# Pooled attention into a SoLU layer on one core: AV in 16 products instead of 24, and the upper halves of w_out on ScalarE

## The chip, the core and the metric

The kernel runs on one core of one Trainium2 chip. The time is the device time of one execution, in microseconds (us). The engines are PE (TensorE, with its weight loads as PEld), DVE (VectorE), ACT (ScalarE), POOL (GpSimd) and SP (SyncE), each with its own queue of instructions that it works through in order. SP issues most DMAs; ACT issues those of the start.

## The reference

```python
def attn(q, k, v):                      # [8, 8, 576, 64], float32
    k_p = k.reshape(B, H, 72, 8, D).mean(axis=3)
    v_p = v.reshape(B, H, 72, 8, D).mean(axis=3)
    scores = 1/sqrt(D) * q @ k_p.T      # 576 x 72 of each head
    a = exp(scores - max); a = a / (sum(a) + 1e-9)
    return a @ v_p
def moe(x, w_in, w_out, g_ln):          # x: [4608, 512] of all heads side by side
    h = x @ w_in                        # [4608, 1024]
    solu = h * softmax(h)
    ln = (solu - mean) / sqrt(var + 1e-6) * g_ln
    return ln @ w_out                   # [4608, 512]
```

The arithmetic is carried in pairs of float16 numbers: each float32 operand is split into an upper half (`hi`, the rounded value) and a rest (`lo`), and a product is the sum of hi·hi, hi·lo and lo·hi.

## The kernel before

There are 36 tiles of 128 rows. Each of the 8 batches has 512 query rows in four tiles of its own; its last 64 rows go with those of its neighbour into a mixed tile, so that four of the 36 tiles work on two batches in halves of 64 rows. Two batches take nine tiles.

For each batch K and V are loaded as eight rows of 64 beside each other (`load_kv`, L205, three DMAs: two of 512 KB, one of 128 KB) and added up by POOL in three steps (`pool_kv`, L237). The pooled V has 8 heads x 72 = 576 rows, which stand in five columns of blocks of 128. `v_hi` (L340, ACT) and `v_lo` (DVE) split it, and `v_put` (L353, POOL, four instructions of 128x512) lays it into the block matrices `vb`, in which zeros (the mask `own`) keep two neighbouring heads apart.

For each tile: `q_hi`, `q_lo`, a DMA transpose `q_T`; `scores` on PE; softmax on DVE and ACT (`s_max` to `e_mul`); `e_hi` (L661, ACT) and `e_lo` (L664, POOL); a DMA transpose `e_T` (L670); `av` (L676, PE); `x_hi`, `x_lo`; `mm1` (L704, 24 products of 512 columns in three parts); the SoLU and its norm (`h_max`, `h_exp`, `z_mul`, `z_cen`, `z_hi`, `z_lo`); two DMA transposes `z_T`; `mm2` (L817, 24 products of 512 columns); `o_evac` and `o_store`. A pair of heads has 144 rows of V, more than the 128 of a block, and lies across two blocks. So `av` takes, for each of the four pairs, two blocks times the three half products: 24 products of 128 columns, 48 of 64 columns in a mixed tile.

At the start the weights w_in and w_out are loaded in four pieces each and bounded, scaled and split: `w_exp`, `w_shift`, `w_bnd`, `w_tail`, `w_sgn`, `w_mul`, then `w_dg` (L533) and `w_hi` (L522) and on PE `w_res` (L543, two buffers `ps_h` shared with `mm1`), then `w_lo`. For w_in `w_hi` is on ACT; for w_out `w_hi` and `w_dg` are on DVE, beside POOL's work. `k_dup` (L302) is ACT's first computation.

The order is planned when the kernel is built: `op(...)` gives every step its engine, a cost in us, a due time (moved by the table `SHIFT`) and what it depends on; `plan` (L886) lays the steps out engine by engine, twelve rounds, and the best plan is issued in its order. A DMA's completion is counted on one of eight counters, taken in turn by every DMA of SP and ACT (`DMAHW0` to `DMAHW7` in the listings below). A DMA that takes a counter whose earlier user hasn't landed waits for it in its queue, and what stands behind it in that queue waits too.

```python
                todo = [(e, et, vt) for e in range(2) for et, vt in PASSES]
                for j, (e, et, vt) in enumerate(todo):
                    nc.tensor.matmul(
                        xp[:, c, lo:hi],
                        lhsT=vb[b % 2][:, vt, c, e].rearrange("p j d -> p (j d)"),
```

## Time and profile before

| what | us |
|---|---|
| median of 3 runs (lowest to highest) | 546.53 (545.97 to 548.0) |
| the profiled execution | 546.37 |
| its span, first to last instruction | 544.6 |
| around the span | 1.77 |
| PE busy | 494.2 (91%) |
| DVE busy | 420.4 (77%) |
| POOL busy | 322.3 (59%) |
| ACT busy | 316.8 (58%) |

The profile is of one execution. An engine's busy time is how long it had an instruction at work; the chain that ended last is followed back from the last instruction, at each step to what released it. The granted clock of TensorE is given as a share of 2.4 GHz. A wait is put down to what came last.

### The profile page before, as it was taken

What the parts mean: (1) busy time and instruction counts of PE and PEld (TensorE: products, weight loads), DVE (VectorE), ACT (ScalarE), POOL (GpSimd) and SP (SyncE); (2) the same over time, 40 slices, a digit from 0 to 9 for tenths busy, and PEclk for the clock granted to TensorE, in tenths of its full rate; (3) what the DMA queues carried; (4) which work ended last, traced back from release to release, by engine and by line L of the source; (5) the groups of instructions that cost most, each with busy time, mean ns of one, the idle gap of its engine ahead of it and who ended that gap; (6) DMA issues with size and microseconds to landing.
All of it is one profiled execution on the core that took longest, in us unless ns stands there. A gap on an engine that the chain in (4) does not pass through costs nothing.

```text
span 544.6 us, 9825 instructions
## 1 busy us (share of the span) xinstructions
PE 494.2 (91%) x3558; PEld 268.2 (49%) x3558; DVE 420.4 (77%) x901; ACT 316.8 (58%) x449; POOL 322.3 (59%) x417
## 2 busy tenths in 40 slices
...
GB/s 329 341 144 181 272 39 65 168 228 166 82 261 177 178 102 159 151 251 117 159 240 163 137 134 158 193 194 89 222 207 176 132 86 124 144 95 82 84 77 78
DMA packets 191936, 86.90 MB, mean 160 GB/s; under 512 B 168336, under 2 KB 176528, under 8 KB 191376
## 3 DMA queue, kind: packets, MB, share of 16 engines
...
q8 instruction: 28, 0.46, 0.4%
q14 instruction: 20, 0.16, 0.1%
...
## 4 chain that ended last, share of the span: by engine, by line
PE 67%; DVE 11%; DMA 10%; issue 4%; ACT 3%; SPq 2%; POOL 2%; ACTq 0%; POOLq 0%; DVEq 0%
PE hp L714 26%; PE op L826 25%; PE xp L684 7%; PE sc L616 3%; DMA vr<-in_v_dram 2%; DMA qr<-in_q_dram 2%; DMA eT<-e 2%; DMA qm<-in_q_dram 2%; DMA qT<-q 2%; PE res_wo L547 1%; PE res_wi L547 1%; DVE z L759 1%; DVE wo L527 1%; DVE m L724 1%; PE kTp L310 1%
## 5 line engine op out<-in xcount | busy, mean ns | idle before, releaser
L714 PE MATMUL hp<-wi,xT 128*128 128x512 f16 x864 | 200.0, 379 | 2.4 <-ACT xT L693 2.4
L826 PE MATMUL op<-wo,zT 128*128 128x512 f16 x864 | 198.7, 379 | 1.7 <-ACT osb L834 1.7
L779 POOL TENSOR_TENSOR z<-z,z 128x512 f16<-128x512 f32 x71 | 82.8, 1180 | 112.6 <-ACT z L773 99.8
L826 PEld LDWEIGHTS <-zT 128*128 128x128 f16 x864 | 83.0, 98 | 96.3 <-issue 2.5
L714 PEld LDWEIGHTS <-xT 128*128 128x128 f16 x864 | 82.7, 98 | 95.5 <-ACT xT L693 3.2
L666 POOL TENSOR_TENSOR e<-e,e 128x576 f16<-128x576 f32 x36 | 48.7, 1353 | 51.3 <-ACT e L662 51.3
L724 DVE TENSOR_REDUCE m<-hp 128x1 f32<-128x1024 f32 x36 | 43.9, 1220 | 24.1 <-PE hp L714 24.0
L735 ACT ACTIVATE z<-hp,nb,Hb 128x1024 f32<-128x1024 f32 x32 | 38.4, 1201 | 39.3 <-DVE nb L727 37.0
L684 PEld LDWEIGHTS <-vb 128*128 128x128 f16 x960 | 51.2, 98 | 10.1 <-DMA eT<-e 3.0
L684 PE MATMUL xp<-eT,vb 128*128 128x128 f16 (+1 forms) x960 | 54.4, 214 | 1.9 <-DMA eT<-e 1.7
L768 ACT ACTIVATE z<-z,sz 128x1024 f32<-128x1024 f32 x36 | 41.2, 1145 | 21.8 <-DVE z L759 21.6
L759 DVE SCALAR_TENSOR_TENSOR z<-hp,rs,z 128x1024 f32<-128x1024 f32 x36 | 46.0, 1279 | 4.0 <-ACT z L735 2.9
L246 POOL TENSOR_TENSOR kr<-kr 128x512 f32<-128x512 f32 (+3 forms) x48 | 42.4, 901 | 8.7 <-DMA kr<-in_k_dram 7.3
L246 POOL TENSOR_TENSOR vr<-vr 128x512 f32<-128x512 f32 (+3 forms) x48 | 42.6, 908 | 6.8 <-DMA vr<-in_v_dram 6.5
L693 ACT ACTIVATE xT<-xp 128x512 f16<-128x512 f32 x36 | 21.4, 594 | 41.7 <-PE xp L684 41.7
L662 ACT ACTIVATE e<-e 128x576 f16<-128x576 f32 x36 | 24.5, 680 | 30.0 <-DVE e L656 29.0
L626 DVE TENSOR_REDUCE mx<-sc 128x8 f32<-128x576 f32 x36 | 27.1, 753 | 18.8 <-PE sc L616 18.2
L773 ACT ACTIVATE z<-z 128x1024 f16<-128x1024 f32 x36 | 37.9, 1054 | 0.9
L792 ACT ACTIVATE junk<-z 128x1024 f16<-128x1024 f32 x36 | 37.5, 1043 | 0.7 <-POOL wor L422 0.7
L355 POOL TENSOR_TENSOR vb<-v,own 128x512 f16<-128x512 f16 x32 | 35.8, 1142 | 1.5 <-ACT v L343 1.5
L834 ACT ACTIVATE osb<-op,f 128x512 f32<-128x512 f32 x36 | 24.5, 681 | 19.4 <-PE op L826 9.2
L616 PE MATMUL sc<-kT,qT 128*128 128x72 f16 (+1 forms) x640 | 27.4, 201 | 5.1 <-DMA qT<-q 4.8
(240 smaller groups left out, 641.6 us busy)
## 6 DMA issues: line engine op xcount, KB each, us to landing
...
kr<-in_k_dram SPq DMA_DIRECT2D x14, 512.0 KB, 4.6
qr<-in_q_dram SPq DMA_DIRECT2D x14, 512.0 KB, 4.2
vr<-in_v_dram SPq DMA_DIRECT2D x14, 512.0 KB, 5.3
wir<-in_moe_w_in_dram ACTq DMA_DIRECT2D x4, 1024.0 KB, 12.0
...
zT<-z SPq DMA_TRANSPOSE x72, 2.8
kr<-in_k_dram ACTq DMA_DIRECT2D x2, 512.0 KB, 3.8
```

What stands on the lines that cost most here:

```text
L246: nc.gpsimd.tensor_tensor(out=dst, in0=src[:, :, :n], in1=src[:, :, n : 2 * n], op=ALU.add)
L616: nc.tensor.matmul(o, lhsT=t["qT"][:, h, lo:hi], rhs=kT[:, x, h * SP : (h + 1) * SP], start=(x == 0), stop=(x == 1),)
L666: nc.gpsimd.tensor_tensor(out=eh[:, 1, :NR], in0=tl[i]["e"], in1=eh[:, 0, :NR], op=ALU.subtract)
L684: nc.tensor.matmul(xp[:, c, lo:hi], lhsT=vb[b % 2][:, vt, c, e].rearrange("p j d -> p (j d)"), rhs=eT[:, et * NC + c + e, lo:hi], start=(j ...
L714: nc.tensor.matmul(hp[:, f], lhsT=xT[:, xt, c], rhs=wi[:, wt, c, f * 512 : (f + 1) * 512], start=(c == 0 and xt == 0 and wt == 0), stop=(c ...
L724: nc.vector.tensor_reduce(out=small(i, "m"), in_=tl[i]["hp"], axis=AX.XY, op=ALU.max)
L735: nc.scalar.activation(z, t["hp"], AF.Exp, bias=t["nb"], scale=hsc(i, 0), accum_out=small(i, "se"))
L759: nc.vector.scalar_tensor_tensor(out=t["z"], in0=t["hp"], scalar=t["rs"], in1=t["z"], op0=ALU.mult, op1=ALU.mult, accum_out=small(i, "sz"),)
L768: nc.scalar.activation(t["zf"], t["zf"], AF.Identity, bias=t["sz"], scale=-float(DFF))
L773: nc.scalar.activation(t["z16"][:, 0], t["zf"], AF.Copy)
L779: eng.tensor_tensor(out=t["z16"][:, 1, fs], in0=t["zf"][:, fs], in1=t["z16"][:, 0, fs], op=ALU.subtract)
L826: nc.tensor.matmul(op_, lhsT=zT[:, zt, c], rhs=wo[:, wt, c], start=(c == 0 and zt == 0 and wt == 0), stop=(c == CO - 1 and zt == 1),)
```

## The change

AV is laid out anew. V is loaded by pairs of heads: of the 144 rows of a pair the first 128 make a block of their own (four blocks, columns 0 to 3 of `vp`), and the last 16 of all four pairs share two more blocks (columns 4 and 5), in which each set of 16 rows stands four times. Their split is laid out so that one product takes hi·hi, hi·lo and lo·hi of the rest at once: the copies of V hold hi or lo (`v_sel` makes the per-partition scale, `v_hi` is now two instructions), those of e hold hi, hi, lo, zero (`e_hi` and `e_lo` are now two instructions each). So a pair takes three products for its block and one for the rest: 16 in all, 32 of 64 columns in a mixed tile. The third piece of V's load becomes eight DMAs of 16 partitions and 64 KB each, `pool_kv` of that piece works on 128 partitions and two columns instead of 64 and one, and `v_put` is three instructions.

`w_hi` and `w_dg` of w_out (and `w_dg` of w_in) move from DVE to ACT. The first two pieces of w_in are loaded into the room of `wo`, and the pool `raw` has 6 buffers instead of 7. The planner gets the new costs, and a surcharge for four kinds of DVE step when POOL is at work (`LOCK`), and the table `SHIFT` is new.

```diff
 SHIFT = {
-    "a_all.k": -7.29,
+    "a_all.k": -21.62,
...
-    raw = ctx.enter_context(tc.tile_pool(name="raw", bufs=7))
+    raw = ctx.enter_context(tc.tile_pool(name="raw", bufs=6))
...
+    PIECES = {"kr": ((0, 2), (2, 4), (4, 5)), "vr": ((0, 2), (2, 4), (4, 6))}
...
+        if which == "vr":
+            pairs = rows.rearrange("(t r) x -> r t x", r=PR)
+            if part < 2:
+                eng.dma_start(t[:, c0:c1], pairs[:P, c0:c1])
+            else:
+                for n in range(8):
+                    eng.dma_start(t[16 * n : 16 * n + 16, c0:c1], pairs[P:, n // 4 :: 2])
...
+    def v_sel(b):
+        st = bat[b]
+        st["ss"] = sm.tile([P, 1], F32, tag="ss", name=f"ss{b}")
+        nc.vector.tensor_scalar(
+            out=st["ss"], in0=sel, scalar1=grp["v", b]["s"], scalar2=None, op0=ALU.mult
+        )
...
+        cs = slice(0, CI) if n == 0 else slice(CI, NV)
+        nc.scalar.activation(
+            st["v2"][:, 0, cs], vp[b % 2][:, cs], AF.Copy,
+            scale=grp["v", b]["s"] if n == 0 else st["ss"],
+        )
...
+    HOME = (("wi", 0), ("wi", 1))
...
-                nc.vector.tensor_scalar(
-                    out=w_dst(nm, c, 0)[:, d], in0=w_f32(nm, c)[:, d],
-                    scalar1=w_scl(nm, 2 * c + d), scalar2=None, op0=ALU.mult,
+                nc.scalar.activation(
+                    w_dst(nm, c, 0)[:, d], w_f32(nm, c)[:, d], AF.Copy,
+                    scale=w_scl(nm, 2 * c + d),
                 )
...
-            nc.vector.tensor_scalar(
-                out=t[:, d], in0=ident, scalar1=w_scl(nm, 2 * c + d), scalar2=None, op0=ALU.mult
-            )
+            nc.scalar.activation(t[:, d], ident, AF.Copy, scale=w_scl(nm, 2 * c + d))
...
+    def e_hi(i, n):
+        m, r_ = e_dst(i)
+        if n == 0:
+            nc.scalar.activation(m[:, 0], e_pair(i)[:, :, :P], AF.Copy)
+        else:
+            nc.scalar.activation(
+                r_[:, :, 0:2], e_pair(i)[:, :, P:].unsqueeze(2).to_broadcast([P, CI, 2, 16]), AF.Copy
+            )
...
-                todo = [(e, et, vt) for e in range(2) for et, vt in PASSES]
-                for j, (e, et, vt) in enumerate(todo):
+                for n, (x, e) in enumerate(((0, c), (1, c), (0, CI + c), (2, 2 * CI + c // 2))):
                     nc.tensor.matmul(
...
+    LOCK = ("w_shift", "w_dg", "h_bat", "h_mix")
```

In the listings that follow a row is a line number, an instruction, and out<-in by the program's names; what it waits for stands in brackets. The first place is ACT's queue at the start of the program, up to its first computation (`vr0` is batch 0's V, `wir` w_in, `kp` the pooled K). Before:

```order
L370 DMA wir1_136<-in_moe_w_in_dram 128x2048
L212 DMA vr0_138<-in_v_dram 128x2x512
L212 DMA vr0_138<-in_v_dram 128x2x512 [waits DMAHW0_49]
L216 DMA vr0_138<-in_v_dram 64x512 [waits DMAHW1_49]
L370 DMA wir2_143<-in_moe_w_in_dram 128x2048 [waits DMAHW2_49]
L370 DMA wir3_145<-in_moe_w_in_dram 128x2048 [waits DMAHW3_49]
L477 DMA g_sb_103<-in_moe_g_ln_dram 128x8x1 [waits DMAHW4_49]
L303 ACT_TABLE_LOAD
L303 ACTIVATE kp_0_87<-kp_0_87 128x5x64 [waits Pool_49]
```

After, from the fourth of V's eight small pieces on:

```order
L240 DMA vr0_140<-in_v_dram 16x2x512 [waits DMAHW4_49]
L240 DMA vr0_140<-in_v_dram 16x2x512 [waits DMAHW5_49]
L240 DMA vr0_140<-in_v_dram 16x2x512 [waits DMAHW6_49]
L240 DMA vr0_140<-in_v_dram 16x2x512 [waits DMAHW7_49]
L240 DMA vr0_140<-in_v_dram 16x2x512 [waits DMAHW0_49]
L424 DMA wir2_152<-in_moe_w_in_dram 128x2048 [waits DMAHW1_49]
L424 DMA wir3_154<-in_moe_w_in_dram 128x2048 [waits DMAHW2_49]
L531 DMA g_sb_104<-in_moe_g_ln_dram 128x8x1 [waits DMAHW3_49]
L333 ACT_TABLE_LOAD
L333 ACTIVATE kp_0_87<-kp_0_87 128x5x64 [waits Pool_49]
```

Twenty DMAs instead of thirteen stand ahead of ACT's first computation, and twelve of them instead of five wait on a counter. The last four small pieces wait for the first two pieces of w_in and the two large pieces of V, which stand eight places earlier; the last two pieces of w_in and `g_sb` wait for small pieces.

The second place is SP's queue around the loads of batch 5 (`vr5` is its V, `qm2` the mixed rows of q, `zT`, `qT`, `eT` the transposes with their tile's number). Before:

```order
L212 DMA vr5_3332<-in_v_dram 128x2x512 [waits DMAHW1_49]
L212 DMA vr5_3332<-in_v_dram 128x2x512 [waits DMAHW2_49]
L216 DMA vr5_3332<-in_v_dram 64x512 [waits DMAHW3_49]
L230 DMA qm2_3339<-in_q_dram 64x8x64 [waits DMAHW4_49]
L230 DMA qm2_3339<-in_q_dram 64x8x64 [waits DMAHW5_49]
L787 DMA_TRANSPOSE zT15_3359<-z16_15_3342 128x8x128 [waits DMAHW6_49,Activation_49]
L842 DMA out_0_dram<-osb13_3354 64x512 [waits DMAHW7_49,Activation_49]
L842 DMA out_0_dram<-osb13_3354 64x512 [waits DMAHW0_49]
L603 DMA_TRANSPOSE qT20_3401<-q16_20_3208 128x8x128 [waits DMAHW1_49,DVE_49,PE_49]
L673 DMA_TRANSPOSE eT17_3407<-e16_1_95 128x10x128 [waits DMAHW2_49,Pool_49]
```

After, where the two large pieces of V and four small ones stand just ahead:

```order
L240 DMA vr5_3319<-in_v_dram 16x2x512 [waits DMAHW7_49]
L240 DMA vr5_3319<-in_v_dram 16x2x512 [waits DMAHW0_49]
L240 DMA vr5_3319<-in_v_dram 16x2x512 [waits DMAHW1_49]
L240 DMA vr5_3319<-in_v_dram 16x2x512 [waits DMAHW2_49]
L857 DMA_TRANSPOSE zT15_3352<-z16_15_3342 128x8x128 [waits DMAHW3_49,Activation_49]
L857 DMA_TRANSPOSE zT15_3352<-z16_15_3342 128x8x128 [waits DMAHW4_49,Pool_49]
L655 DMA_TRANSPOSE qT20_3407<-q16_20_3141 128x8x128 [waits DMAHW5_49,DVE_49,PE_49]
L745 DMA_TRANSPOSE eT18_3433<-e16_0_95 128x10x128 [waits DMAHW6_49,Pool_49]
```

Ten DMAs of V instead of three stand ahead of the transposes, and the last small pieces wait on the counters of the large ones.

The third place is where w_out's scale `sg_wo` has been found. Before, on DVE (`nb` and `pz` belong to tile 1's SoLU):

```order
L507 TENSOR_SCALAR sg_wo<-g_sb,sw_wo 128x8
L538 TENSOR_SCALAR dg_wo_682<-ident,sg_wo 128x128 x2
L527 TENSOR_SCALAR wo<-wor_255,sg_wo 128x512 x2
L727 TENSOR_SCALAR nb_689<-m_649,Hb_390 128x1
L742 TENSOR_SCALAR pz_699<-nb_689 128x1
```

After, on ACT (`z_622` is tile 0's SoLU, `q_4` a split of q, `sg_wo_645` signs of w_out, `xT` AV's result):

```order
L805 ACTIVATE z_622,se_623<-hp_540,nb_618,Hb_420 128x1024
L473 ACTIVATE sg_wo_645<-wor_298 128x1024
L592 ACTIVATE dg_wo_650<-ident,sg_wo 128x128 x2
L581 ACTIVATE wo<-wor_268,sg_wo 128x512 x2
L643 ACTIVATE q_4_679<-qm_391,sq('m', 0)_487 128x8x64
L473 ACTIVATE sg_wo_691<-wor_296 128x1024
L763 ACTIVATE xT_696<-xp_655 128x512
L581 ACTIVATE wo<-wor_271,sg_wo 128x512 x2
```

The scale's first users leave DVE's queue and stand in ACT's, between tile 0's exponential and the work of the next tiles.

## Rows read from the trace of the kernel before

**Rows 1.** The page's first part: busy time, share of the span, instructions.

```profile
PE 494.2 (91%) x3558; PEld 268.2 (49%) x3558; DVE 420.4 (77%) x901; ACT 316.8 (58%) x449; POOL 322.3 (59%) x417
```

**Rows 2.** Stretches: length, busy us of PE, PEld, DVE, ACT, POOL; clock, DMA, GB/s.

```profile
60.00:80.00 20.00, 10.10 (x34) 4.88 (x33) 16.65 (x31) 7.21 (x9) 17.63 (x21) 0.72 0.44 128
80.00:100.00 20.00, 17.83 (x88) 8.92 (x87) 18.22 (x48) 12.30 (x18) 5.15 (x4) 0.77 0.28 59
...
220.00:240.00 20.00, 20.00 (x166) 10.84 (x165) 18.63 (x40) 13.49 (x20) 17.78 (x24) 1.00 0.82 192
...
100.00:520.00 420.00, 417.02 (x3128) 228.25 (x3126) 333.21 (x742) 256.44 (x377) 252.92 (x338) 1.00 0.71 157
```

**Rows 3.** The chain that ended last: start us, us, what.

```profile
154.59 1.34 PE xp L684 x24
...
466.44 1.40 PE xp L684 x48
```

**Rows 4.** In order of time: start, us, engine, line, tiles [idle <-releaser].

```profile
9.24 0.39 ACTq L477 DMA_DIRECT2D g_sb<-in_moe_g_ln_dram  x1
...
9.66 1.28 ACT L303 ACT_TABLE_LOAD   x1 [9.66 <-DMA qr<-in_q_dram]
...
11.65 1.14 ACT L381 ACTIVATE u_wi<-wir 128x1024 f32<-128x1024 f32 x1 [0.23 <-DMA wir<-in_moe_w_in_dram]
...
15.48 2.94 POOL L246 TENSOR_TENSOR vr<-vr 128x512 f32<-128x512 f32 x2 [5.17 <-DMA vr<-in_v_dram]
```

**Rows 5.** The chain that ended last, 15 to 79 us.

```profile
15.31 8.82 DMA qT<-q
...
57.64 8.83 DMA qm<-in_q_dram
...
70.99 2.13 DVE dg_wo L538 x2
73.12 5.58 DVE wo L527 x2
```

**Rows 6.** In order of time: first mm1, exponential of tile 1, upper halves.

```profile
51.72 5.35 PE L714 MATMUL hp<-wi,xT 128*128 128x512 f16 x24 [0.78 <-ACT xT L693]
...
78.92 1.20 ACT L735 ACTIVATE z<-hp,nb,Hb 128x1024 f32<-128x1024 f32 x1 [7.65 <-DVE nb L727]
...
83.15 0.88 DVE L527 TENSOR_SCALAR wo<-wor,sg_wo 128x512 f16<-128x512 f32 x2
```

**Rows 7.** Groups by line: shapes xcount | busy us, mean ns | idle before.

```profile
L693 ACT ACTIVATE xT<-xp 128x512 f16<-128x512 f32 x36 | 21.4, 594 | 41.7 <-PE xp L684 41.7
...
L662 ACT ACTIVATE e<-e 128x576 f16<-128x576 f32 x36 | 24.5, 680 | 30.0 <-DVE e L656 29.0 <-DMA qT<-q 1.0
...
L303 ACT ACTIVATE kp<-kp 128x320 f32<-128x320 f32 x8 | 3.7, 464 | 6.1 <-POOL kp L246 6.0
```

**Rows 8.** SP's queue in order of time, around the loads of batch 5.

```profile
274.86 1.08 SPq L212 DMA_DIRECT2D vr<-in_v_dram  x2
275.99 0.50 SPq L216 DMA_DIRECT2D vr<-in_v_dram  x1
...
280.19 1.26 SPq L787 DMA_TRANSPOSE zT<-z  x1
```

**Rows 9.** DMA issues: queue, count, KB of each, median us to landing.

```profile
kr<-in_k_dram SPq DMA_DIRECT2D x14, 512.0 KB, 4.6
...
vr<-in_v_dram SPq DMA_DIRECT2D x14, 512.0 KB, 5.3
...
kr<-in_k_dram SPq DMA_DIRECT2D x7, 128.0 KB, 5.4
...
eT<-e SPq DMA_TRANSPOSE x36, 3.5
```

**Rows 10.** A transpose of e on SP's queue, and the AV that waits for it.

```profile
284.23 1.37 SPq L673 DMA_TRANSPOSE eT<-e  x1
...
289.18 1.51 PE L684 MATMUL xp<-eT,vb 128*128 128x128 f16 x24 [1.49 <-DMA eT<-e]
```

More of the change, by code (lines that the diff above doesn't have):

```diff
@@ L39 @@
+    "a_scale.v": 9.35,
+    "av": 0.2,
+    "e_T": -35.76,
+    "e_hi": 0.79,
+    "e_lo": 5.3,
     "e_mul": 8.03,
-    "e_rec": -0.94,
+    "e_rec": -1.23,
     "e_sum": -0.71,
-    "g_all": 3.07,
-    "g_max": -7.17,
-    "g_par": -0.13,
-    "h_bat": -7.02,
-    "h_exp": 10.98,
-    "h_max": -0.22,
-    "h_mix": 5.51,
-    "k_T": 6.76,
-    "k_dup": -0.29,
-    "k_hi": -10.23,
-    "k_lo": 0.24,
-    "load_kv": -3.11,
-    "load_q": -2.51,
-    "mm1": 1.89,
-    "mm2": 17.69,
-    "n_f": -6.27,
@@ L58 @@
-    "n_u": 0.28,
-    "o_evac": 1.32,
-    "o_store": 19.63,
-    "pool_kv": 2.95,
-    "q_T": 0.49,
-    "q_hi": 1.92,
-    "q_lo": -0.97,
-    "s_exp": -0.25,
-    "s_max": -1.15,
-    "s_scale": -18.57,
-    "s_sub": -15.94,
-    "v_hi": -8.55,
-    "v_put": -9.46,
-    "w_all.wi": 4.98,
-    "w_all.wo": 0.91,
-    "w_bnd.wi": 21.74,
-    "w_bnd.wo": 11.25,
-    "w_dg.wi": -1.48,
-    "w_dg.wo": -9.92,
-    "w_exp.wi": 3.61,
-    "w_exp.wo": -0.14,
-    "w_hi.wi": 1.44,
-    "w_hi.wo": 0.16,
@@ L103 @@
-    "z_cen": -3.7,
-    "z_hi": 2.72,
-    "z_lo": -0.21,
-    "z_mul": -2.61,
-    "z_var": -13.56,
+    "g_all": -0.73,
+    "g_max": -5.26,
+    "g_par": -5.5,
+    "h_bat": -1.1,
+    "h_exp": 16.71,
+    "h_max": -0.53,
+    "h_mix": 5.41,
+    "h_nb": 12.08,
+    "k_T": 7.39,
+    "k_dup": -5.05,
+    "k_hi": -18.66,
+    "k_lo": -0.62,
+    "load_g": 2.84,
+    "load_kv": 13.41,
+    "load_q": -1.14,
+    "load_qm": 5.52,
+    "mm1": 6.24,
+    "mm2": 17.69,
+    "n_f": -7.69,
+    "n_u": 12.93,
@@ new lines @@
+    "o_evac": 2.32,
+    "o_store": 18.59,
+    "pool_kv": 3.34,
+    "q_T": 8.03,
+    "q_hi": 1.3,
+    "q_lo": -1.2,
+    "s_exp": 17.42,
+    "s_max": -1.08,
+    "s_scale": -27.59,
+    "s_sub": -21.86,
+    "scores": -1.24,
+    "v_hi": -10.93,
+    "v_put": -10.2,
+    "v_sel": 0.46,
+    "w_all.wi": -1.93,
+    "w_all.wo": -2.71,
+    "w_bnd.wi": 7.93,
+    "w_bnd.wo": 11.25,
+    "w_dg.wi": -3.34,
+    "w_dg.wo": -11.46,
+    "w_exp.wi": -0.35,
+    "w_exp.wo": 1.16,
+    "w_hi.wi": 2.97,
@@ new lines @@
+    "w_hi.wo": -0.18,
+    "w_lo.wi": -8.77,
+    "w_lo.wo": -3.33,
+    "w_load": 2.82,
+    "w_mul.wi": -23.05,
+    "w_mul.wo": 8.49,
+    "w_par.wi": 15.48,
+    "w_par.wo": -0.82,
+    "w_res.wi": -11.03,
+    "w_res.wo": 1.46,
+    "w_rmax.wi": -9.29,
+    "w_rmax.wo": -8.02,
+    "w_sgn.wi": -4.96,
+    "w_sgn.wo": 9.07,
+    "w_shift.wi": -1.82,
+    "w_shift.wo": 1.26,
+    "w_tail.wi": 0.65,
+    "w_tail.wo": -13.63,
+    "wi_scale": 3.13,
+    "wo_scale": -7.86,
+    "x_hi": -0.18,
+    "x_lo": -12.0,
```

200 lines of the change are left out of this document (109 added, 91 removed).

## The prediction

> **What bounds the kernel now.** I read the page's busy times first, then the busy times by stretch, then the chain that ended last, and then, where PE stands idle, the engines in order of time. By the page PE is busy 494.2 of 544.6 us, DVE 420.4 [rows 1]. By stretch this falls into two programs. From 100 to 520 us PE is busy 417.0 of 420 us [rows 2]; nothing else is as full, and the chain there is a row of products. What leaves PE in that stretch leaves the time, until another engine is full. The nearest is DVE with 333.2 of 420, and 18.63 of 20 in its fullest stretch [rows 2]. Before 100 us PE is not the bound: 10.10 of 20 us from 60 to 80, at a mean granted clock of 0.72 (a mixture of the two levels 2.4 and 1.2 GHz), while DVE has 16.65 and then 18.22 [rows 2]. There DVE, its waits and POOL beside it set the pace.
>
> **AV.** A tile's 24 products take 1.34 us in the chain, a mixed tile's 48 take 1.40 [rows 3]: 55.8 and 29.2 ns each. Eight fewer in 32 tiles are 32 x 8 x 0.0558 = 14.3 us, sixteen fewer in four mixed tiles 4 x 16 x 0.0292 = 1.9: 16.2 in all. Two of the tiles (2 x 0.45) come before PE is full, which leaves 15.3 us on the path. The trace shows no product over a block of rests, but its shapes are those of the others, so the price holds.
>
> The Trainium skill, TensorE: Matmul & The Clock Gate, section Back-to-back issue gap, has about 81 ns for such a product of 128 columns in a stream of weight loads and products; the row has 55.8, and the measurement decides. By the page's figure an estimate of the saving would be 32 x 8 x 0.081 + 4 x 16 x 0.081 = 25.9 us.
>
> **What the rests add to the other engines.** e_hi was one instruction of 0.680 us; now one of 512 columns, nearest 0.594, and one of 128, at most the 0.464 of 320 columns [rows 7]: up to 0.38 us more of ACT for each tile, 13.6 in all, on an engine that is busy 256.4 of 420 us from 100 to 520 [rows 2]. On POOL (252.9 of 420) e_lo grows by an instruction, v_put shrinks from four to three and the sums of V's last piece double; all of this is under a us for each tile, and PE's work on other tiles hides it. If that cover were gone, e's transposition, and so AV, would come about 0.5 us later. I take 0.
>
> **V's loads and SP's queue.** Three DMAs of V become ten. In the trace two took SP 1.08 us, the third 0.50 [rows 8], and the next transposition stood behind 1.6 us of V. A large piece of V lands 5.3 us after its issue [rows 9]. The last two small pieces wait on the counters of the two large ones, so the queue is free again no earlier than about 5.3 + 2 x 0.50 = 6.3 us: 4.7 more, in six batches that are loaded while PE is full. Behind it stand z, q and e transposes, and PE for them. The trace has one place where e is late: its transpose was issued at 284.23, right behind such loads, and AV began at 289.18 after PE had waited 1.49 us [rows 10]; had it landed in the median 3.5 us [rows 9], PE would not have waited. PE lost almost nothing elsewhere (3.0 of 420 us, rows 2), so mostly there is room. Bounds: 0, and 6 x 1.6 = 10 if a third of each delay is seen. I take +3, nearer the first, since the plan puts z's transposes, not e's, behind most of these loads.
>
> In the trace a piece of 128 KB lands after 5.4 us, one of 512 KB after 4.6 [rows 9]. The Trainium skill, DMA: Bandwidth & Descriptors, section Rules for kernel authors, speaks against such a split: join small transfers, under 64 KB is mostly overhead. Rows and rule agree that a small piece saves no time in landing; by the rule alone the term would be the upper bound, 10, and the sum 7 us worse.
>
> **DVE when PE is faster.** 420 us become about 405 for the same 333 us of DVE, so its fullest stretch of 18.63 in 20 [rows 2] becomes 19.3. Some steps will come late: bounds 0 and 5, I take +2.
>
> **The start, first half: a loss.** ACT's first computation was at 9.66, when the DMA of g_sb, waiting for q's second half, had been issued at 9.24 [rows 4]. Now small pieces wait in ACT's queue for w_in's pieces and V's. V's first large piece landed about 15.5, when POOL began on it, and the second by about 16.9, in the middle of POOL's two steps of 2.94 [rows 4]. Behind that stand four issues (the last small piece, two of w_in, g_sb) of some 0.4 us [rows 4]: ACT begins at about 18.5, 8.9 us later. Not all of it is lost, because q's first transposition took 8.82 us from 15.31 on [rows 5], behind w_in's pieces; now it is issued at about 24.3 (18.5 + 1.28 for the table + 0.46 for k_dup + 1.14 for an exponent step + 0.7 for q_hi [rows 4, 7] + 2.2 on DVE), those pieces have landed, and at the 3.5 of e's transpose [rows 9] it is there at about 27.8 instead of 24.1: +3.7. The new order gives ACT about 3.3 us more between w_in's scale and the first mm1 (two exponent steps of w_out, second halves of e_hi and v_hi, w_dg), so the first mm1 starts some 7 us after its 51.72 [rows 6].
>
> **The start, second half: a gain.** DVE stood waiting for qm's DMA, 8.83 us from 57.64 to 66.47 [rows 5], since its issue was behind K's and V's loads. Now qm is issued ahead of them. Then DVE spent 2.13 + 5.58 = 7.7 us on one pair of w_dg and two halves of w_hi [rows 5], beside a busy POOL; two such halves took 0.88 once POOL was idle [rows 6]. Tile 1's exponential waited 7.65 us for what stood behind them on DVE [rows 6]. On ACT the same four steps cost 2 x 0.46 + 2 x 0.594 = 2.1 [rows 7], 5.6 less. Adding up DVE's steps in the new order I get w_out's scale at about 68.4 instead of 71.0, so w_hi is through at 70.5 instead of 78.7: 8.2 earlier. Part is given back: ACT, at 7.21 and 12.30 of 20 us [rows 2], takes 4 x 2.1 = 8.4 us there, and two buffers serve w_res and mm1 in turn. Half of 8.2 is 4; less 1, because the first half's delay may not be hidden to the end, I take -3 for the whole start. Bounds: -10 (8.2 and the 2.6 of the scale, nothing given back) and +8 (the first half's 7 and an us of lower clock).
>
> **The sum.** -15.3 + 3 + 2 - 3 = -13.3 from the profiled execution's 546.37 is 533.1; its time stands 0.16 under the median of 546.53, so I say 533.
>
> **The rivals.**
> - *The whole gain of the start.* DVE's waits beside POOL vanish and ACT hides its loads: -16.2 - 10 + 2 = about 522. For it: the 7.7 us of rows 5. Against: ACT's 8.9 us.
> - *The start loses.* The delay of 7 reaches the second half and PE falls to 1.2 GHz again after idling, as it did from 60 to 80: -15.3 + 3 + 2 + 8 = -2.3, 544. For it: ACT's queue. Against: PE was half idle there before, too, so a late mm1 costs little of itself.
> - *Slower: SP's queue becomes the bound.* Every delay of 4.7 us by V's ten DMAs is seen by PE at six batches, 28 us: -15.3 - 3 + 28 = +10, about 556. It is a loss from (15.3 + 3) / 6 = 3.1 us a batch on. For it: the place of rows 10. Against: PE's 417 of 420.
> - *DVE becomes the bound,* and half of AV's gain stays: -7.7 - 3 + 5 = -5.7, 541.
> - *A product costs more than the chain shows,* by the figure cited above: 25.9 instead of 15.3 in the sum, -23.9, 522. No row of the trace bears it out.
>
> **How the numbers follow.** Forecast 0.60; the start's whole gain 0.14; the start loses 0.12; SP 0.06; DVE 0.06; the product's price 0.02. A measurement of this kernel tells about 0.5% from no change, here 543.8 to 549.3. The forecast, the two cases at 522, DVE's and a third of the start's loss lie below: 0.60 + 0.14 + 0.02 + 0.06 + 0.04 = 0.86. Two thirds of the start's loss are no change, 0.08; SP is slower, 0.06. The range leaves out SP, part of the start's loss and the best of its gain: 521 to 544.
>
> **What would show it.** Right: AV's row at 16 products in about 0.9 us, 32 in 0.93; PE still busy 99% from about 100 us on, that stretch shorter by 10 to 15 us; ACT's table load near 18.5; the first mm1 near 58, w_out's first w_hi near 70. Wrong: PE waits on eT, zT or qT summing to over 10 us, each with V's small pieces before it on SP (the slower rival); DVE at 19 of 20 for long with PE waiting for it; or a first mm1 after 62, with PE's clock at 0.5 once mm2 has begun.

## The result and the profile after

The changed kernel takes 539.19 us (median of 4 runs, 537.49 to 540.55) beside 546.51 of the kernel before: a ratio of 0.986, 95% interval 0.9825 to 0.9895. That is 7.3 us less, where 13.5 were forecast (533 in a range of 521 to 544). The profiled execution took 538.74 us, its span is 537.0. Medians are of all runs of a kernel, ratios of its fast runs alone; only the last experiment (best) has a slow run, of 535.66 us, and the median of its other five is 530.51.

The page of the kernel after, busy time of each engine; the answer to [rows 1]:

```profile
PE 475.5 (89%) x3238; PEld 251.6 (47%) x3238; DVE 417.0 (78%) x895; ACT 330.3 (62%) x510; POOL 323.5 (60%) x445
```

PE has 18.7 us less to do, but the span is only 7.6 us shorter: PE stands idle for 61.5 instead of 50.4 us. Where, the stretches tell (columns as in [rows 2]). First the start of the kernel before, which was not shown:

```profile
0.00:100.00 100.00, 58.23 (x347) 31.71 (x348) 82.71 (x149) 53.80 (x64) 64.62 (x74) 0.90 0.62 189
```

Then the same and the rest, after:

```profile
0.00:100.00 100.00, 49.33 (x331) 28.79 (x332) 78.54 (x137) 55.31 (x78) 60.81 (x74) 0.93 0.65 189
...
60.00:80.00 20.00, 11.00 (x86) 6.96 (x87) 19.27 (x29) 6.71 (x11) 13.81 (x15) 0.79 0.43 108
80.00:100.00 20.00, 17.69 (x116) 9.99 (x116) 18.73 (x44) 18.49 (x32) 11.30 (x14) 0.87 0.25 46
...
100.00:520.00 420.00, 414.92 (x2860) 218.09 (x2859) 337.74 (x758) 270.28 (x427) 260.12 (x368) 1.00 0.80 166
```

Idle time of PE before 100 us: 41.8 before, 50.7 after. From 100 to 520 us: 3.0 before, 5.1 after. The start can be cut at the first mm1, as the prediction cuts it. Before:

```profile
0.00:51.72 51.72, 22.52 (x167) 13.52 (x167) 39.58 (x63) 30.66 (x34) 36.99 (x47) 1.00 0.79 255
51.72:100.00 48.28, 35.71 (x180) 18.19 (x181) 43.13 (x87) 23.14 (x30) 27.63 (x27) 0.79 0.45 118
```

After:

```profile
0.00:63.65 63.65, 23.22 (x169) 14.33 (x169) 44.19 (x70) 31.39 (x38) 39.27 (x49) 0.98 0.87 268
63.65:100.00 36.35, 26.11 (x162) 14.46 (x163) 34.35 (x68) 23.92 (x41) 21.53 (x26) 0.85 0.27 51
```

Up to the first mm1 PE is idle for 29.2 us before and 40.4 after; from there to 100 us for 12.6 and 10.2. AV's own row, in the chain that ended last (start, us, what), answers to [rows 3]:

```profile
142.93 0.89 PE xp L755 x16
...
234.12 0.93 PE xp L755 x32
```

The groups of instructions by line give AV 39.8 us of PE in all, 54.4 before. Set against the sum of the prediction, in us of the profiled span:

| part | forecast | rows of both traces |
|---|---|---|
| AV's products | -15.3 | 39.8 - 54.4 = -14.6 |
| PE's waits from 100 to 520 us (SP's queue +3, DVE +2) | +5 | 5.1 - 3.0 = +2.1 |
| start, first half: PE idle up to the first mm1 | +1 | 40.4 - 29.2 = +11.2 |
| start, second half: PE idle from there to 100 us, and PE's other work | -4 | 10.2 - 12.6 - 4.1 = -6.4 |
| end, behind 520 us | 0 | +0.2 |
| sum | -13.3 | -7.5 |

The 4.1 are what is left of PE's 18.7 beside AV: with the same instructions, work done at a higher mean clock (0.93 instead of 0.90 before 100 us), most of it `w_res` of w_out (12.6 us of PE instead of 16.2). The two lines of the start make +4.8 together, where -3 was forecast: the miss is the start, and in it the first half. Its rows, in order of time (start, us, engine, line, tiles [idle before <-releaser]); they answer to [rows 4 to 6]:

```profile
5.75 12.52 ACTq L240 DMA_DIRECT2D vr<-in_v_dram  x8
...
19.73 1.28 ACT L333 ACT_TABLE_LOAD   x1 [19.73 <-DMA vr<-in_v_dram]
...
63.65 5.80 PE L784 MATMUL hp<-wi,xT 128*128 128x512 f16 x24 [0.47 <-ACT xT L763]
...
67.48 5.72 DVE L699 TENSOR_SCALAR r<-r 128x8 f32<-128x8 f32 x1
...
79.37 2.06 DVE L561 TENSOR_SCALAR sg_wo<-g_sb,sw_wo 128x8 f32<-128x8 f32 x1
...
82.06 1.40 ACT L581 ACTIVATE wo<-wor,sg_wo 128x512 f16<-128x512 f32 x2
```

ACT's table load came at 19.73 (18.5 forecast, 9.66 before). The first mm1 came at 63.65 (some 58.7 forecast, 51.72 before). w_out's first upper half came at 82.06, where the forecast had both through by 70.5. And a step of DVE on 8 columns, e_rec, lasted 5.72 us, where its median is 0.17.

### The profile page after: what moved, and what is told of

It is laid out like the page before. It is cut to its first block, busy times and chain, and to the rows that moved or that the text cites. A ratio compares the mean times of both kernels' runs of the same rounds, so it can differ in the third digit from the quotient of the medians.

```text
span 537.0 us, 9335 instructions
## 1 busy us (share of the span) xinstructions
PE 475.5 (89%) x3238; PEld 251.6 (47%) x3238; DVE 417.0 (78%) x895; ACT 330.3 (62%) x510; POOL 323.5 (60%) x445
## 4 chain that ended last, share of the span: by engine, by line
PE 52%; DVE 13%; DMA 11%; POOL 8%; issue 4%; ACT 4%; SPq 2%; POOLq 0%; ACTq 0%; DVEq 0%
PE hp L784 20%; PE op L896 20%; DMA vr<-in_v_dram 6%; PE xp L755 4%; POOL vr L276 2%; PE sc L668 2%; DVE z L829 2%; DMA eT<-e 2%; POOL z L849 1%; DVE r L699 1%; PE res_wi L599 1%; POOL kr L276 1%; DMA kr<-in_k_dram 1%; PE res_wo L599 1%; DVE q L647 1%
## 5 line engine op out<-in xcount | busy, mean ns | idle before, releaser
L784 PE MATMUL hp<-wi,xT 128*128 128x512 f16 x864 | 196.1, 380 | 0.6 <-ACT xT L763 0.6
L896 PE MATMUL op<-wo,zT 128*128 128x512 f16 x864 | 194.2, 380 | 2.2 <-ACT osb L904 1.7
L849 POOL TENSOR_TENSOR z<-z,z 128x512 f16<-128x512 f32 x71 | 84.0, 1198 | 83.8 <-ACT z L843 71.7
L734 POOL TENSOR_TENSOR e<-e,e 128x512 f16<-128x512 f32 x36 | 43.6, 1211 | 27.6 <-ACT e L725 27.5
L276 POOL TENSOR_TENSOR vr<-vr 128x512 f32<-128x512 f32 (+1 forms) x48 | 49.8, 1052 | 12.4 <-DMA vr<-in_v_dram 10.1
L829 DVE SCALAR_TENSOR_TENSOR z<-hp,rs,z 128x1024 f32<-128x1024 f32 x36 | 46.1, 1281 | 5.3 <-ACT z L805 4.4
L755 PE MATMUL xp<-eT,vb 128*128 128x128 f16 (+1 forms) x640 | 39.8, 219 | 6.4 <-POOL vr L276 3.2
L755 PEld LDWEIGHTS <-vb 128*128 128x128 f16 x640 | 36.5, 100 | 15.4 <-issue 4.2
L725 ACT ACTIVATE e<-e 128x512 f16<-128x512 f32 x36 | 22.5, 625 | 28.5 <-DVE e L708 28.4
L767 DVE SCALAR_TENSOR_TENSOR xT<-xp,xT 128x512 f16<-128x512 f32 x36 | 24.7, 686 | 11.9 <-ACT xT L763 11.6
```

The costliest lines, as they stand in the source:

```text
L276: nc.gpsimd.tensor_tensor(out=dst, in0=src[:, :, :n], in1=src[:, :, n : 2 * n], op=ALU.add)
L734: nc.gpsimd.tensor_tensor(out=m[:, 1], in0=e_pair(i)[:, :, :P], in1=m[:, 0], op=ALU.subtract)
L755: nc.tensor.matmul(xp[:, c, lo:hi], lhsT=vb[b % 2][:, x, c].rearrange("p j d -> p (j d)"), rhs=eT[:, e, lo:hi], start=(n == 0), stop=(n == 3),
L784: nc.tensor.matmul(hp[:, f], lhsT=xT[:, xt, c], rhs=wi[:, wt, c, f * 512 : (f + 1) * 512], start=(c == 0 and xt == 0 and wt == 0), stop=(c ...
L829: nc.vector.scalar_tensor_tensor(out=t["z"], in0=t["hp"], scalar=t["rs"], in1=t["z"], op0=ALU.mult, op1=ALU.mult, accum_out=small(i, "sz"),)
L849: eng.tensor_tensor(out=t["z16"][:, 1, fs], in0=t["zf"][:, fs], in1=t["z16"][:, 0, fs], op=ALU.subtract)
```

## The experiments

Two theories on the start: A, it is lost in ACT's queue behind V's small pieces; B, it is lost on DVE, held beside POOL. Two more questions: what AV's products are worth in the end, and whether SP's queue and the new order took a part. The kernel before was run again beside the experiments, with medians of 546.46 to 546.98; single runs of a kernel lie 2 to 4 us apart, so a difference of 2 us between two medians is no more than the scatter. Wherever the listing says nothing else, the order of the operations is that of the changed kernel.

### What AV is worth: av24 and b_av16

```diff
-for n, (x, e) in enumerate(((0, c), (1, c), (0, CI + c), (2, 2 * CI + c // 2))):
+todo = ((0, c), (1, c), (0, c), (1, c), (0, CI + c), (2, 2 * CI + c // 2))
+for n, (x, e) in enumerate(todo):
...
-    rhs=eT[:, e, lo:hi], start=(n == 0), stop=(n == 3),
+    rhs=eT[:, e, lo:hi], start=(n in (0, 2)), stop=(n in (1, 5)),
```

> The changed kernel with 24 products in AV again: the first two of each block are computed twice, the second time with a fresh start of the sum, so that the output stays and the order, the loads and the other engines' work are those of 16. If PE is the bound after 100 us and a product costs what the chain shows, 32 x 8 x 0.0558 + 4 x 16 x 0.0292 = 16.2 us come back and the whole is about 554. If DVE, SP or the loads had become the bound after the change, a part of it would be hidden: under 10 us, below 549.

549.48 us, 10.3 more than the changed kernel and 2.7 more than the kernel before (ratio 1.0051, 1.0032 to 1.0071). The stretches of av24, the start and the full part:

```profile
0.00:100.00 100.00, 49.45 (x351) 29.85 (x352) 77.45 (x136) 54.45 (x77) 61.07 (x73) 0.93 0.64 189
100.00:520.00 420.00, 418.15 (x3103) 228.03 (x3102) 331.22 (x745) 266.35 (x421) 255.72 (x363) 1.00 0.79 164
```

PE is busy 490.9 us, 15.4 more: the price of a product was right. But PE now idles 1.9 us from 100 to 520 instead of 5.1, so 3.2 of the 15.4 had been given back as waits. That leaves 12 us between the two profiled executions, and 10.3 between the medians. And with 24 products the new kernel is the slower one: all that the change does beside AV costs about 2.7 us. The forecast had +2 for it, by two errors of opposite sign (below).

In the kernel before, the other way:

```diff
-todo = [(e, et, vt) for e in range(2) for et, vt in PASSES]
+todo = [(e, et, vt) for e in range(2) for et, vt in PASSES[:2]]
```

> The kernel before, with 16 of its 24 products in AV: the third pass, the lower halves of V against the upper halves of e, is left out; all else, the order and the loads too, is the kernel before. If the chain's 55.8 ns a product are what a product costs on the path, the whole falls by 15.3 to 16.2 us from 546.5 to about 531. If DVE or a transfer is next as soon as PE has less to do, a part of it is lost, and the whole falls by about 10, to 536, as the changed kernel rose by 10 with 24 products.

By `PASSES` the pass that is left out is the other one, e's lower halves against V's upper ones; the number of products is the same.

540.74 us: only 5.7 less (0.9894, 0.9867 to 0.9921), less than either case. The stretch from 100 us on, and two of PE's waits:

```profile
100.00:520.00 420.00, 410.39 (x2858) 216.71 (x2856) 337.81 (x746) 256.83 (x379) 254.98 (x340) 1.00 0.72 159
...
237.16 3.63 PE L714 MATMUL hp<-wi,xT 128*128 128x512 f16 x16 [1.11 <-ACT xT L693]
289.82 1.89 PE L684 MATMUL xp<-eT,vb 128*128 128x128 f16 x16 [2.84 <-DMA eT<-e]
```

PE idles 9.6 us there instead of 3.0, and the place of [rows 10] waits 2.84 instead of 1.49 us. In the old order, what stood just in time for a full PE is late as soon as PE has less to do. The order was not planned anew for 16 products here.

### What the new order is worth: old_table

The table `SHIFT` of the kernel before in the changed kernel.

> The changed kernel with one part undone: the table that sets the planner's order is that of the kernel before; the operations, their durations and the loads are those of the changed kernel. The kernel before with 16 products fell by 5.7 us where the changed kernel rose by 10.3 with 24. If the new table is what lets the rest of AV's saving through, the whole is 4 to 6 us longer, 542 to 545. If the new table only moves the work, and the start's loss comes from it, the whole is 2 to 5 us shorter, 534 to 537.

550.8 us, 11.6 more than the changed kernel, and slower than the kernel before (1.0072, 1.0042 to 1.0101). PE idles 12.1 us from 100 to 520 us, 7.0 more than in the changed kernel; another 1.5 us of idle time come before 100 us, and PE's work takes 3.6 us longer. The longest wait from 100 us on stands behind V's loads. SP's queue and the AV that waits:

```profile
396.87 5.53 SPq L232 DMA_DIRECT2D vr<-in_v_dram  x8
402.58 1.26 SPq L849 DMA_TRANSPOSE zT<-z  x1
403.94 1.18 SPq L904 DMA_DIRECT2D out_dram<-osb  x2
405.20 1.56 SPq L737 DMA_TRANSPOSE eT<-e  x1
...
410.41 1.05 PE L747 MATMUL xp<-eT,vb 128*128 128x128 f16 x16 [3.22 <-DMA eT<-e]
```

So the order is a part of this change: under the old table the change loses.

### What SP's hold costs: v_16

```diff
-    eng.dma_start(t[16 * n : 16 * n + 16, c0:c1], pairs[P:, n // 4 :: 2])
+    for c in range(1 if b == 0 else 2):
...
+        eng.dma_start(t[16 * n : 16 * n + 16, cs], pairs[P:, ts])
```

Here `cs` and `ts` are one chunk each from the second batch on.

> The changed kernel, but from the second batch on the small pieces of V are sixteen of 32 KB instead of eight of 64 KB, each chunk by itself; the bytes are the same. In the changed kernel eight such issues held SP 6.32 us at 59.16; sixteen wait for the landings of the eight before, and hold it some 5 to 6 us more for each of seven batches. If SP's hold is on the path as the prediction priced it (3 us for 4.7 us in each of six batches), the whole is 3 to 5 us longer, 542 to 544; by the slower rival, where every us of it is seen, over 25 us longer; if it is hidden, within 1.5 us of 538.7.

565.94 us (1.034, 1.0306 to 1.0375), 26.7 more, about what the slower rival had. One of the seven places, and PE's work behind it:

```profile
416.91 9.61 SPq L243 DMA_DIRECT2D vr<-in_v_dram  x16
426.62 1.26 SPq L860 DMA_TRANSPOSE zT<-z  x1
427.98 1.36 SPq L748 DMA_TRANSPOSE eT<-e  x1
...
431.59 1.86 PE L758 MATMUL xp<-eT,vb 128*128 128x128 f16 x16 [4.72 <-DMA eT<-e]
433.25 7.21 PE L899 MATMUL op<-wo,zT 128*128 128x512 f16 x24
```

PE's stretches there (columns as in [rows 2]):

```profile
431.00:434.00 3.00, 2.41 (x18) 1.99 (x19) 0.00 (x0) 0.51 (x2) 0.00 (x0) 0.50 0.89 231
434.00:441.00 7.00, 7.00 (x41) 3.27 (x39) 3.65 (x11) 2.55 (x6) 6.13 (x11) 0.78 1.16 197
```

In the changed kernel the small pieces hold SP for 46.2 us in seven batches (5.24 to 8.61 each), here for 72.9 (9.61 to 11.61): 26.7 more, and the whole is 26.7 longer. That the two are the same number is chance. PE's idle time from 100 to 520 us goes from 5.1 to 20.4, 15.3 us for 26.7 of hold; nearly all of the rest is PE's longer busy time, 10.8 us. Behind the wait of 4.72 us the granted clock is 0.50 (1.2 GHz) from 431 to 434 and 0.78 from 434 to 441, and mm2's 24 products took 7.21 us instead of 5.34. So the hold of 6.6 us for each batch is hidden but for a few us in all, and over half of what v_16 adds to it is seen as waits. These are two points: where between 6.6 and 10.4 us for each batch the waits begin wasn't tried. The longest wait in the changed kernel from 100 us on stands behind the pieces of V that held SP from 394.50 on:

```profile
394.50 6.66 SPq L240 DMA_DIRECT2D vr<-in_v_dram  x8
401.26 1.27 SPq L857 DMA_TRANSPOSE zT<-z  x1
402.63 1.38 SPq L745 DMA_TRANSPOSE eT<-e  x1
...
406.29 1.05 PE L755 MATMUL xp<-eT,vb 128*128 128x128 f16 x16 [2.18 <-POOL vr L276]
```

The wait is put down to a sum of V on POOL, which AV doesn't read; e's transpose, at its median of 3.5 us, landed at about 406.1, and is the likelier cause.

### ACT's queue at the start: v_sp0 and v_spq

```diff
 for n, _, _ in order:
-    ops[n][3](*ops[n][4])
+    fn, args = ops[n][3], ops[n][4]
+    if fn is load_kv and args[1:] == (0, "vr", 2):
+        continue
+    fn(*args)
+    if fn is load_g:
+        load_kv(nc.sync, 0, "vr", 2)
```

> The changed kernel, but the eight small pieces of V of the first batch are issued from SP, which stands idle at the start, instead of from ACT. Theory A (the start is lost in ACT's queue, where those eight issues took 12.52 us from 5.75 on): ACT's table load falls from 19.73 to about 10 to 12, the first mm1 from 63.65 to about 55 to 57, and the whole from 538.7 to about 533. Theory B (the start is lost on DVE beside POOL, where e_rec took 5.72 us at 67.48 and w_out's scale 2.06 at 79.37): ACT begins earlier, but the first w_hi of w_out stays near 80 and the whole within 2 us of 538.7.

538.63 us, no difference. It doesn't decide between the theories: the counters that a DMA waits for go round over SP's and ACT's DMAs together, so ACT's own loads came to wait instead, and the table load stood at 17.32, behind w_in. The first mm1 came 2.3 us earlier, at 61.32, but PE's waits from 100 to 520 us rose from 5.1 to 6.9. The second experiment issues them from SP behind q's first transposition (`fn is q_T and args[0] == 0`).

> The changed kernel, but the eight small pieces of V of the first batch are issued from SP, behind q's first transposition; nothing else is moved. Theory A: ACT waits for few landings, its table load comes at about 10 instead of 19.73, q's first transposition is issued near 16 instead of 25.4, the first mm1 comes at 55 to 58 instead of 63.65, and the whole is 4 to 6 us shorter, 533 to 535. Theory B: mm1 comes earlier, but e_rec is held on DVE until POOL is done, w_out's scale comes within 2 us of its 79.4, and the whole stays within 1.5 us of 538.7.

537.22 us (0.983, 0.9798 to 0.9862), 2 less than the changed kernel. ACT's and PE's first steps, and e_rec:

```profile
8.37 1.28 ACT L333 ACT_TABLE_LOAD   x1 [8.37 <-DMA qr<-in_q_dram]
...
59.13 3.19 PE L784 MATMUL hp<-wi,xT 128*128 128x512 f16 x14 [0.50 <-ACT xT L763]
...
63.55 5.72 DVE L699 TENSOR_SCALAR r<-r 128x8 f32<-128x8 f32 x1
```

The stretches of v_spq:

```profile
0.00:100.00 100.00, 53.86 (x358) 31.19 (x359) 78.25 (x145) 58.82 (x85) 64.59 (x76) 0.93 0.68 193
100.00:520.00 420.00, 412.04 (x2833) 215.75 (x2832) 334.84 (x750) 267.77 (x422) 256.42 (x365) 1.00 0.81 165
```

ACT starts 11.4 us earlier, mm1 4.5 earlier, the end 2. PE's idle time before 100 us falls by as much as mm1 moves, from 50.7 to 46.1, but from 100 to 520 us it rises from 5.1 to 8.0: behind the start nothing was planned anew, and a part of the gain comes back as waits. Theory A holds for half of PE's added idle time at the start. The first mm1 is still 7.4 us behind its 51.72; q's second transposition now stands behind SP's small pieces (issued at 26.56) and ACT's work ahead of mm1 has grown. How these two share the 7.4 wasn't tried.

### DVE beside POOL: rec_stt, rec_fold, pool_less

```diff
-nc.vector.tensor_scalar(
-    out=r, in0=r, scalar1=1e-9, scalar2=1.0 / S14, op0=ALU.add, op1=ALU.mult
+nc.vector.scalar_tensor_tensor(
+    out=r, in0=r, scalar=1e-9, in1=c14, op0=ALU.add, op1=ALU.mult
...
```

> The changed kernel, but e_rec's first step and the scale of w_out with gamma are SCALAR_TENSOR_TENSOR with a second tensor instead of TENSOR_SCALAR; same places in the order. Theory B: the 5.72 us of e_rec at 67.48 and the 2.06 us at 79.37 become about 0.2 us each, w_out's first w_hi goes from 82 to about 75, and the whole falls by about 5 us to 534. Theory A: the steps get short, too, but DVE waits elsewhere, and the whole stays within 1.5 us of 538.7. A third case: this form is held beside POOL just as long, then nothing changes at all.

539.41 us: the third case. In this form e_rec is held just as long. DVE's row, and the last of POOL's instructions beside it:

```profile
66.98 5.71 DVE L705 SCALAR_TENSOR_TENSOR r<-r,c 128x8 f32<-128x8 f32 x1
...
71.41 1.25 POOL L280 TENSOR_TENSOR vr<-vr 128x512 f32<-128x512 f32 x1
```

DVE's step ends at 72.69, 0.03 us after POOL's five instructions in a row, which end at 72.66. Then e_rec's first step was taken out:

```diff
-nc.vector.tensor_scalar(
-    out=r, in0=r, scalar1=1e-9, scalar2=1.0 / S14, op0=ALU.add, op1=ALU.mult
-)
+pass
...
-nc.vector.tensor_tensor(
-    out=e.rearrange("p (a h r) -> p a h r", a=2, r=SP), in0=s_view(i),
-    in1=tl[i]["r"].unsqueeze(3).to_broadcast([P, 2, HB, SP]), op=ALU.mult,
+nc.vector.scalar_tensor_tensor(
+    out=e.rearrange("p (a h r) -> p a h r", a=2, r=SP), in0=s_view(i), scalar=S14,
+    in1=tl[i]["r"].unsqueeze(3).to_broadcast([P, 2, HB, SP]), op0=ALU.mult, op1=ALU.mult,
...
-nc.vector.tensor_scalar(out=sg, in0=g_sb, scalar1=sw, scalar2=None, op0=ALU.mult)
+nc.vector.tensor_tensor(out=sg, in0=g_sb, in1=sw.to_broadcast([P, CO]), op=ALU.mult)
```

> The changed kernel without e_rec's first step: its factor, a power of two, goes into e_mul, which becomes SCALAR_TENSOR_TENSOR (the 1e-9 falls away, since a sum of exponentials less their maximum is 1 or more), and w_out's scale with gamma is a TENSOR_TENSOR against a repeated column. Theory B (DVE stands behind POOL in these small steps): the 5.72 us at 67.48, the 1.32 us at 58.11 and most of the 2.06 us at 79.37 are gone, w_out's first w_hi comes near 75 instead of 82, and the whole is 4 to 6 us shorter, 533 to 535. Theory A (ACT's queue at the start): DVE's steps are short, but PE still begins as late, and the whole is within 1.5 us of 538.7. Third case: another step of DVE is held to the same end of POOL's work, at 73.17; then that step shows some 5 us and the whole stays.

537.41 us (0.9837, 0.9801 to 0.9873): 1.8 less, where theory B had 4 to 6: the third case again, at the next step. In rec_fold, DVE's w_tail and POOL's last row:

```profile
67.85 6.48 DVE L458 SCALAR_TENSOR_TENSOR u_wo<-wor,u_wo 128x1024 int32<-128x1024 int32 x1
...
71.99 1.25 POOL L276 TENSOR_TENSOR vr<-vr 128x512 f32<-128x512 f32 x1
```

POOL ends at 73.24, w_tail 1.09 later, about its own time (1.2 us elsewhere). With e_rec gone, w_tail is held in its place; what is won is e_rec's first step itself (DVE is busy 397.2 instead of 417.0 us, over all 36 tiles). PE's idle time before 100 us falls by 1.1 us only (50.7 to 49.5). Last, a part of POOL's work was taken away:

```diff
+if (b, which, lvl) == (1, "vr", 0) and part < 2:
+    return
 nc.gpsimd.tensor_tensor(
     out=dst, in0=src[:, :, :n], in1=src[:, :, n : 2 * n], op=ALU.add
```

> The changed kernel without the first sums of the two large pieces of V of batch 1 on POOL (left out, so this batch's V is summed over fewer rows); these are POOL's two steps of 1.25 us at 68.62 and 71.92, between and behind which e_rec was held on DVE. If DVE is held until POOL's row of work has ended, e_rec falls from 5.72 to about 3.2 us, ending with w_mul at about 70.7. If it is held for another reason (its own wait, a queue), it stays at 5.7. The whole: up to 2.5 us shorter, since w_out's scale comes that much earlier.

537.17 us, with one round of runs (0.9814, 0.9764 to 0.9865). K's piece landed later here and POOL began 2 us later, so e_rec slipped through and w_tail was held:

```profile
68.20 5.01 DVE L460 SCALAR_TENSOR_TENSOR u_wo<-wor,u_wo 128x1024 int32<-128x1024 int32 x1
...
70.01 2.11 POOL L478 TENSOR_TENSOR wor<-u_wo,sg_wo 128x1024 f32<-128x1024 f32 x1
```

POOL's row now ends with w_mul at 72.12, and w_tail again 1.09 later, at 73.21. In four kernels the step of DVE that is held at this place comes free with the last of five instructions of POOL in a row, whichever step it is. That DVE's steps wait for POOL, theory B's mechanism, is shown.

That a hold lasts to the end of POOL's row is not the rule, though. The scale at 79.37 in the changed kernel came free at 81.43, 0.03 us after one instruction of POOL, and POOL's next followed that one without a gap:

```profile
79.28 2.12 POOL L476 TENSOR_TENSOR wor<-u_wo,sg_wo 128x1024 f32<-128x1024 f32 x1 [6.12 <-ACT sg_wo L473]
81.36 2.64 POOL L276 TENSOR_TENSOR vr<-vr 128x256 f32<-128x256 f32 x3
```

Of e_rec's 36 first steps in the changed kernel 15 were held, and each ended 0.03 us after an instruction of POOL. Fourteen lasted 0.34 to 1.32 us, until the one instruction ended beside which they had begun, and behind twelve of these POOL went on at once; only the one at 67.48 was held through four ends of instructions. Why POOL kept its turn there isn't shown. Nor is the price of this hold: every kernel here, the one before too, has one step of DVE of 5.0 to 6.5 us at the start (half of w_hi, 5.26 at 73.05, in the kernel before; w_tail, 6.47 at 63.02, in best). The change didn't add such a step, and it didn't remove it.

The Trainium skill, GPSIMD Engine Reference, section Key points, says that POOL shares SBUF interfaces with DVE, in contention with DVE's instructions in a 2-port mode or with two SBUF inputs. The rows agree as far as they go: both forms of e_rec and w_tail were held, e_rec's second form and w_tail with two such inputs; whether e_rec's first form ran in a 2-port mode the trace doesn't say.

### Both cures, and the undone part: fold_spq, wo_dve, best

> The changed kernel with both: the small pieces of V of the first batch from SP behind q's first transposition, and e_rec's first step gone. If the two losses are one behind the other, they add up: 9 to 11 us less than 538.7, about 529. If they are beside each other (either alone hides the other), the two together give 5 to 8 us, while each alone gives under 2.

534.7 us (0.9781, 0.9743 to 0.9819): 4.5 less than the changed kernel. Alone the two gave 2.0 and 1.8, so by medians they add up, as the first case had it, but at about half of its size; each alone is within the scatter of single runs.

Then w_out's w_dg and w_hi back on DVE, at the same places:

```diff
-nc.scalar.activation(
-    w_dst(nm, c, 0)[:, d], w_f32(nm, c)[:, d], AF.Copy,
-    scale=w_scl(nm, 2 * c + d),
+nc.vector.tensor_scalar(
+    out=w_dst(nm, c, 0)[:, d], in0=w_f32(nm, c)[:, d],
+    scalar1=w_scl(nm, 2 * c + d), scalar2=None, op0=ALU.mult,
...
```

> The changed kernel with one part undone: w_out's diagonals (w_dg) and upper halves (w_hi) on DVE as before the change, at the places that the new order has for them. If the four steps are dear on DVE because POOL is busy beside them, as before the change (7.7 us for one pair of w_dg and two halves of w_hi), the whole is 3 to 6 us longer, about 543. If ACT, busy 18.49 of 20 us from 80 to 100, has become what w_out waits for, it is 1 to 3 us shorter, about 537.

546.93 us (1.0011, 0.9983 to 1.0039): 7.7 more, somewhat over the first case. The first pair of w_dg, and upper halves, two each, on DVE:

```profile
81.98 1.84 DVE L595 TENSOR_SCALAR dg_wo<-ident,sg_wo 128x128 f32<-128x128 f32 x2
...
84.93 1.48 DVE L581 TENSOR_SCALAR wo<-wor,sg_wo 128x512 f16<-128x512 f32 x2
...
98.30 0.87 DVE L581 TENSOR_SCALAR wo<-wor,sg_wo 128x512 f16<-128x512 f32 x2
```

The last upper halves on ACT in the changed kernel:

```profile
92.28 1.41 ACT L581 ACTIVATE wo<-wor,sg_wo 128x512 f16<-128x512 f32 x2
```

So this part of the change is a gain, but not for the reason given. The first four steps cost DVE 1.84 + 1.48 = 3.3 us here, not 7.7, and on ACT 2.1 as forecast (0.69 and 1.40), and the last halves are shorter on DVE than on ACT. What the rows show to be lost is their turn: among DVE's other steps the first two halves end at 86.41 instead of 83.46 and the last two at 99.17 instead of 93.69, and PE is busy 44.62 us before 100 instead of 49.33.

Last, fold_spq with the scale of w_out on ACT:

```diff
-nc.vector.tensor_tensor(out=sg, in0=g_sb, in1=sw.to_broadcast([P, CO]), op=ALU.mult)
+nc.scalar.activation(sg, g_sb, AF.Copy, scale=sw)
```

> The changed kernel with both cures of the start (the small pieces of V of the first batch on SP behind q's first transposition; e_rec's first step folded into e_mul), and the scale of w_out with gamma on ACT, where POOL doesn't hold it: DVE's 2.05 us beside w_mul become an ACT step of about 0.3. If w_out's scale is still on the path at the start, the whole is 1 to 2 us below the 534.7 without that last part, about 533; if something else has become late there, it is the same 534.7.

531.89 us (0.9685, 0.9644 to 0.9725; single runs from 527.07 to 535.66), the fastest kernel here, 7.3 below the median of the changed one. The step, and the first upper halves, 6.9 us earlier than in the changed kernel:

```profile
73.36 0.30 ACT L561 ACTIVATE sg_wo<-g_sb,sw_wo 128x8 f32<-128x8 f32 x1 [1.09 <-DVE sw_wo L556]
...
75.17 1.40 ACT L581 ACTIVATE wo<-wor,sg_wo 128x512 f16<-128x512 f32 x2
```

Of these 7.3 us the last step has 2.8 between medians of runs that scatter by as much. It brought the first upper halves only 0.9 us ahead of fold_spq's 76.09, and best's profiled execution is the longer one (533.78 us beside 532.21), so its size is not settled. The sum of the three is clear: no run of best reaches the 537.49 of the changed kernel's shortest.

## Why the prediction was half right

**What bounds the kernel:** right for the full part: PE was busy 414.9 of 420 us after, too.

**AV, -15.3:** right in its price (-14.6 in the rows; 15.4 us of PE with the products put back) and in its place; 10 to 12 us of it reach the whole. 320 products more cost 15.4 us, 48 ns each over both sorts. So the rival at 522, by the 81 ns of the Trainium skill (TensorE: Matmul & The Clock Gate, section Back-to-back issue gap), is refuted.

**DVE when PE is faster, +2, and SP's queue, +3:** together 5, measured 2.1 more of PE's waits. DVE's fullest stretch from 100 us on came out as estimated (19.23 of 20 us, from 380 to 400, for 19.3). The mechanisms are real, but their cover is the new order: in the old order the same eight products fewer brought 6.6 us of new waits from 100 to 520 us (b_av16), and the changed kernel under the old table idles 12.1 us there. For SP the forecast argued from three of the right things, the hold (6.3 forecast, 6.32 measured at 59.16), who stands behind it, and where the plan puts e; but it took the cost for a slope from zero on. The present hold costs at most a few us, and the next 26.7 us of it 15.3 of waits and 10.8 of longer products (v_16).

**The start, -3:** this term failed; it measured +4.8, nearer to the rival "the start loses" (+8). The step that failed is the price of its first half: a delay of some 7 us at the first mm1, of which 1 was charged, because PE was half idle there before, too. The delay was 11.9 us, and PE's idle time up to mm1 grew by 11.2. ACT's table load (19.73 for 18.5) and the landing of q's first transposition (28.57 for 27.8) were nearly right; from that landing to mm1 it took 35.1 us instead of 27.6, 7.5 more where the forecast had 3.3. And a late mm1 was not hidden: when v_spq brought it 4.5 us forward, PE's idle time before 100 us fell by 4.5.

The second half was to gain 4 and measured -6.4, of which 2.3 are idle time and 4.1 PE's higher clock. Its steps did not come as forecast, though. w_out's upper halves were to be through 8.2 us earlier than at 78.7; their first pair ended at 83.46. The sentence that failed here is "Adding up DVE's steps in the new order I get w_out's scale at about 68.4". The scale was there at 81.43, 13 us later. Of these, 5 are mm1's further delay (63.65 for 58.7). Behind mm1 8 more came, and 7.4 of them are two holds beside POOL, e_rec's (5.72 us for 0.17) and the scale's (2.06 for 0.22). No hold is named in that sum. The trace of before had shown DVE's steps held beside POOL, [rows 5], and the forecast booked their move to ACT as 7.7 us that vanish. But the hold belongs to POOL's work, not to the step: now e_rec is held, and without it w_tail.

Cures for what could be named gave 4.5 us (ACT's queue and e_rec together; 2.0 and 1.8 alone) and 2.8 (the scale), by medians, together 7.3, about the 7.8 us between forecast and measurement. That they come to the same figure is no proof that nothing else is in it: a part of e_rec's gain lies behind the start, and in best PE still idles 44.2 us before 100 us, beside 41.8 in the kernel before. Which of ACT's added work and q's second transposition makes mm1 late beyond ACT's late beginning stays open.

**The rest, e_hi, e_lo, v_put at 0:** nothing speaks against it: from 100 to 520 us ACT had 13.8 us more and POOL 7.2, and none of PE's waits there is put down to e_hi, e_lo or v_put.

**The range and the chances:** 539.2 lies in the range, and the time fell by 1.4%, over the 0.5% that can be told apart. That it lies there is in part luck: the start came out 7.8 us dearer than forecast and AV 0.7, the two terms for DVE and SP 2.9 cheaper. The rival nearest to it, "DVE becomes the bound" (541), isn't what happened: from 100 to 520 us DVE was busy 337.7 of 420, and PE's longest wait on it took 0.38 us. Of the signs to tell the forecast right by, AV's rows, PE's 99% and nearly the table load came; the first mm1 near 58, the first w_hi near 70 and a full stretch 10 us shorter didn't. Of the three to tell it wrong by, half of one came: a first mm1 after 62 us, without the clock of 0.5 once mm2 had begun (1.00 from 100 us on).
